# Six short blocks at the start, every load on one queue, and a new plan for a fused convolution and two-layer feed-forward kernel

## The chip, the cores and the metric

The kernel runs on one core of one Trainium2 chip. The metric is the device time of one execution in microseconds (us), as the median of several runs; smaller is better.

## The reference, cut to what matters

```
out[s] = sum_k softmax(weight_gen[s])[h, k] * x[s - 6 + k]       # 7 taps, 8 heads, 192 channels, zero padded
h  = out @ w_in1                                                  # 192 -> 2048
g  = (a0 + a1 h + a2 h^2 + a3 h^3) / (1 + |b0||h| + |b1| h^2)
x2 = g @ w_out1                                                   # 2048 -> 192
h  = x2 @ w_in2                                                   # 192 -> 2048
y  = (h * clip(h + 3, 0, 6) / 6) @ w_out2                         # 2048 -> 192
```

There are 8192 tokens (two sequences of 4096). The weights arrive as 64-bit floats and are turned into 32-bit ones on the chip.

## The kernel before, in words

**Tiling.** 128 partitions hold 128 runs of 64 consecutive tokens, so one row across the partitions is 128 tokens. A block is 256 tokens (2 rows) or 512 tokens (4 rows): `BL = [2, 2] + [4] * 15`. A unit `u` is two rows of convolution. For each block and each of 16 groups of 128 hidden columns, the kernel runs layer one, then layer two. A slice is 512 columns of one PSUM bank: one hidden group for a 512-token block, two for a 256-token block. There are 256 slices in all, 8 for a short block and 16 for a long one.

**Convolution.** Every four rows (a chunk) are loaded with their weights (`load_gen`, `load_chunk`), the softmax is done in five steps, and each row takes two multiplications (`conv_mul`, L177, on POOL) and two reductions (`conv_sum`, L192, on DVE). `x_dup`, `xT`, `x_hi` and `x_lo` transpose a unit on PE and split it in a high and a low part, so that two reduced-precision matmuls stand for one exact one.

**Layer one.** `in1` is five matmuls for each hidden group (L279). The function of h is then computed in one of two ways: a slice that is "whole" takes `act_v`, `act_s` (ACT) and `dve_q` (DVE, L321); the others take `act_u`, `act_w`, `act_q` (ACT) and `pool_q` (POOL, L341). `whole` is true for two slices of three. All slices share `act_l`, `dve_t`, `dve_t2`, `act_ln`, `act_exp`, `dve_hi`, `pool_m`, `dve_d` and `pool_lo`. `out1` (L418 to L422) adds five matmuls for each hidden group into `y1`, one tile of two PSUM banks for each block.

**Handover.** When `out1` of a block is complete, `mid_y`, `mid_f`, `mid_head`, `head_lo`, `mid_tail` and `tail_lo` fold and split `y1` into the input of layer two (`xh1`, `xl1`). The next block's first `out1` waits until `y1` is free again, that is, for `tail_lo` (L262).

**Layer two.** `in2` is five matmuls for each hidden group, `act_r2` and `dve_g2` follow, and `out2` (L454) is two or four rows of 16 matmuls each for the result, evacuated by `evac` and stored from SP's queue.

**Weights.** 28 jobs load a piece of a weight and decode it: `low`, `scale` (ACT), `join`, `sign` (DVE), `hi` (ACT) and `lo` (L532, mostly POOL). The first two jobs are loaded from ACT's queue, all others from SP's.

**The order.** `plan()` is a list scheduler in the kernel itself: every step has an engine, a cost, a due time and the steps it needs, and the order of each engine's instructions is what it returns. The due times come from the constants (`T`, `JP0`, `C1`, ...). Where the plan leaves PE idle ahead of the second block's layer two, it puts matmuls of the identity (`idle_mm`, L402), which compute nothing that is used.

Of the kernel before, what the change touches and what calls it, by code (L numbers as in the profile page):

```python
# [19 lines left out]
def kernel(  # L20
# [25 lines left out]
    BL = [2, 2] + [4] * 15  # L46
    B0 = [sum(BL[:b]) // 2 for b in range(len(BL))]
    BT = [n * P for n in BL]
    BV = [n // 2 for n in BL]
    BF = [GW // n for n in BT]  # L50
    BMAX = max(BT)
    UB = [(b, v) for b, n in enumerate(BV) for v in range(n)]
# [52 lines left out]

    def load_chunk(c):
        t = two.tile([P, ROWS, D], F32, tag="x", name="x")
        first = c * CT - (K - 1)
        neg = max(0, -first)
        cut_at = ROWS - 2 if c == 0 else ROWS  # L110
        segs = [(0, P, neg, cut_at)]
        if neg:
            for b in range(B):
                p = b * S // R
                nc.gpsimd.memset(t[p : p + 1, 0:neg, :], 0.0)
                segs += [(p + 1, p + 16, 0, neg), (p + 16, p + S // R, 0, neg)]
        if cut_at < ROWS:
            segs.append((0, P, cut_at, ROWS))
        for p0, p1, r0, r1 in segs:
            src = bass.AP(  # L120
                tensor=xf.tensor,
                offset=xf.offset + (first + p0 * R + r0) * D,
                ap=[[R * D, p1 - p0], [1, (r1 - r0) * D]],
            )
            nc.sync.dma_start(out=t[p0:p1, r0:r1].rearrange("p r d -> p (r d)"), in_=src)
        xch[c] = t
# [35 lines left out]
    NH = 4  # L162
    NS = 3
# [35 lines left out]
    def x_dup(u):  # L199
        t = xc[u]  # L200
        nc.scalar.activation(out=t[:, :, D:], in_=t[:, :, P:D], func=AF.Copy)

    def xT(u):
        t = xc.pop(u)
        ps = bank(("xT", u), [P, 2, HB], "xT")
        for s in range(2):
            nc.tensor.transpose(ps[:, 0, s * P : (s + 1) * P], t[:, s, 0:P], ident)  # L207
            nc.tensor.transpose(ps[:, 1, s * P : (s + 1) * P], t[:, s, P : 2 * P], ident)
        xps[u] = ps

    def x_hi(u):
        b, v = UB[u]
        if v == 0:
            xin[0, b] = [
                two.tile([P, 2, BMAX], F32R, tag=n, name=n)[:, :, : BT[b]] for n in ("xh0", "xl0")
            ]
        xh = xin[0, b][0]
        nc.scalar.activation(out=xh[:, :, v * HB : (v + 1) * HB], in_=xps[u], func=AF.Copy)

    def x_lo(u):  # L220
        b, v = UB[u]
        xh, xl = (t[:, :, v * HB : (v + 1) * HB] for t in xin[0, b])
        nc.vector.tensor_tensor(out=xl, in0=xps.pop(u), in1=xh.bitcast(F32), op=ALU.subtract)
# [3 lines left out]
    def mid_y(b):  # L227
        ysb[b] = one.tile([P, BMAX], F32, tag="ys", name="ys")[:, : BT[b]]
        for h in range(2):
            nc.scalar.activation(  # L230
                out=ysb[b][h * 64 : (h + 1) * 64],
                in_=y1[b][(1 - h) * 64 : (2 - h) * 64, 1, : BT[b]],
# [3 lines left out]
    def mid_head(b):  # L236
        n = BT[b]
        xin[1, b] = [
            one.tile([P, 2, BMAX], F32R, tag=t, name=t)[:, :, :n]
            for t in ("xh1", "xl1")  # L240
        ]
        nc.scalar.activation(out=xin[1, b][0][:, 0, :], in_=y1[b][:, 0, :n], func=AF.Copy)

    def head_lo(b):
        xh, xl = xin[1, b]
        nc.vector.tensor_tensor(
            out=xl[:, 0, :], in0=y1[b][:, 0, : BT[b]], in1=xh[:, 0, :].bitcast(F32),
            op=ALU.subtract,
        )

    def mid_f(b):
        c = y1[b][:, 1, : BT[b]]
        nc.vector.tensor_tensor(out=c, in0=c, in1=ysb.pop(b), op=ALU.add)

    def mid_tail(b):
        nc.scalar.activation(
            out=xin[1, b][0][:, 1, :], in_=y1[b][:, 1, : BT[b]], func=AF.Copy
        )

    def tail_lo(b):  # L260
        xh, xl = xin[1, b]
        nc.vector.tensor_tensor(  # L262
            out=xl[:, 1, :], in0=y1[b][:, 1, : BT[b]], in1=xh[:, 1, :].bitcast(F32),
            op=ALU.subtract,
        )

    def mm_in(i, xs, f, dst):
# [4 lines left out]
            (w["hi"], xh[:, 0, :]),  # L272
            (w["hi"], xl[:, 0, :]),
            (wst[i], xh[:, 1, :]),
            (wst[i], xl[:, 1, :]),
            (w["lo"], xh[:, 0, :]),
# [18 lines left out]
    def in1(sl):  # L295
        b, _ = SL[sl]
        h1[sl] = bank(("in1", sl), [P, GW], "h1")
        for i, n in enumerate(fs_of(sl)):
            mm_in(0, xin[0, b], n, cols(b, h1[sl], i))

    def whole(sl):
        return sl < QN and sl % QK in QS
# [89 lines left out]
    y1 = {}  # L392

    def open_y1(b):
        if b not in y1:
            y1[b] = ps_y.tile([P, 2, GW], F32, tag="y1", name="y1")

    def idle_mm(n):
        first = not y1
        open_y1(0)  # L400
        for i in range(n):
            nc.tensor.matmul(  # L402
                out=y1[max(y1)][:, i % 2, GW - P :], lhsT=ident, rhs=ident,
                start=first and i < 2, stop=False, skip_group_check=True,
            )

    def out1(sl):
        b, q = SL[sl]
        open_y1(b)
        a, c = y1[b][:, 0, : BT[b]], y1[b][:, 1, : BT[b]]  # L410
# [3 lines left out]
        for i, n in enumerate(fs_of(sl)):  # L414
# [5 lines left out]
            mm(out=c, lhsT=ws, rhs=gh, start=st, stop=False, **kw)  # L420
# [26 lines left out]
    def out2(b, v, part):  # L447
        if part == 0:
            y2[b, v] = bank(("out2", b, v, 0), [P, 2, D], "y2")
        for n in range(part * NF // 4, (part + 1) * NF // 4):  # L450
            q, i = divmod(n, BF[b])
            for s in range(2):
# [9 lines left out]
    def evac(b, v):  # L462
        u = B0[b] + v
        o = two.tile([P, 2, D], F32, tag="osb", name="osb")
        nc.scalar.activation(out=o, in_=y2.pop((b, v)), func=AF.Copy)
        nc.sync.dma_start(out=of[:, u * 2 : u * 2 + 2, :], in_=o)
# [106 lines left out]
    def job_step(key, n, e=None):  # L573
        eng = nc.vector if e == "DVE" else nc.gpsimd
        if n == "load":
            kind, a = key[0], key[1:]
            j = {"in": job_in, "pair": job_pair, "o1": job_out1, "o2": job_out2}[kind](*a)
            job_load(j, nc.scalar if key in order[:2] else nc.sync)
# [16 lines left out]
        else:  # L595
            for _, l in j["cuts"]:
                if l:
                    l(eng)
# [12 lines left out]
    CP = 0.946  # L611
    KP = 0.118
    WIN = 41.47
    SWL = 14.0
    BETA = 0.009
    C1 = -13.219
    CV = 3.155
    SM = 5.662
    XQ = -11.533
    XTP = 2.81  # L620
    XH = -3.719
    O1 = 4.488
    UM = 4.195
    I2 = -0.894
    SPR = 0.852
    R2 = -0.625
    O2 = 4.833
    OS = 0.939
    EV = 10.467
    IDLE = 0.2  # L630
    ops = {}
# [7 lines left out]
    def add(name, eng, cost, prio, fn, *a, after=(), take=(), lat=None):  # L639
# [8 lines left out]
    ]  # L648
    done = {}
    for n, key in enumerate(order):  # L650
        p = JP0 + min(n, 14) * JPT + max(0, n - 14) * JPU - (30.0 if n < 2 else 0.0)
        f64, split = WS == 2, key[0] != "o2"
        sz = 1.0 if key[0] in ("in", "pair") else 0.75
        last = ("job", key, "lo" if split else "sign" if f64 else "load")

        def step(k, eng, cost, prev, take=(), lat=None, also=[]):
            op(
                ("job", key, k), eng, cost, p - LP * (k == "load"), lambda e=None, key=key, k=k: job_step(key, k, e),
                ([("job", key, prev)] if prev else []) + also, take, lat,
            )  # L660

        flex = (("POOL", 1.25 * sz, 0.0), ("DVE", 0.62 * sz, PEN))
        step("load", "SP", 2.0 * sz, None, [("big", ST, [last])] if f64 or split else [], 2.0)
# [11 lines left out]
    for u, (b, v) in enumerate(UB):  # L675
        t0 = S0[b] * T - (BV[b] - 1 - v) * 8 * T
        c = u // 2
        if u % 2 == 0:
            t = t0 - CV * T
            add("gen", "SP", 0.6, t - XQ * T if c else X0P, load_gen, c, lat=2.0,  # L680
                take=[("wg", 2, [("softmax_m", c)])])
            add("load", "SP", 3.7, t - XQ * T + 1.0 if c else X0P + 0.5, load_chunk, c, lat=2.0,
                take=[("x", 2, [("conv_mul", 2 * c + 1, 1, 1)])])
            soft = (("POOL", 0.55, 0.0), ("DVE", 1.0, PEN))
# [5 lines left out]
                take=[("wk", 2, [("conv_mul", 2 * c + 1, 1, 1)])])  # L690
        for i in range(2):
# [257 lines left out]
```

## Time and profile before

| what | us |
|---|---|
| median of 3 runs | 1308.34 |
| lowest, highest | 1306.3, 1308.44 |
| the profiled execution, its own time | 1305.82 |
| its span in the trace | 1304.0 |
| PE busy in the span | 1281.1 |
| DVE busy | 1143.5 |
| ACT busy | 1069.3 |
| POOL busy | 984.3 |

The span lies inside the time of the execution, which is 1.8 us longer. PE is TensorE, DVE is VectorE, ACT is ScalarE, POOL is GpSimd, SP is SyncE, which only issues DMAs here. PE's busy time contains the identity matmuls of `idle_mm`.

### The profile page before, as it was taken

The page shows a single profiled execution, that of the slowest core. Times are in us where ns is not written, and L with a number is a line of the kernel's source. Part 1 is how long each engine was busy: PE and PEld are TensorE (multiplying, and loading weights), DVE is VectorE, ACT ScalarE, POOL GpSimd, SP SyncE. Part 2 cuts the span into 40 slices and gives each one's busy share as a digit, 9 for nine tenths or more (in the row PEclk, how much of TensorE's full clock was granted, in tenths as well). Part 3 has the DMA queues.
Part 4 walks back from the last instruction along what each step waited for, and adds up shares of the span by engine and source line. Part 5 has one row for each costly group of instructions (what it writes and reads, how often), then busy time and mean ns, then how long its engine had stood idle before and what let it go on. Part 6 is the DMA issues. An engine that isn't in the chain of part 4 may idle for free.

```text
span 1304.0 us, 18918 instructions
## 1 busy us (share of the span) xinstructions
PE 1281.1 (98%) x6640; PEld 1127.2 (86%) x6640; DVE 1143.5 (88%) x1774; ACT 1069.3 (82%) x1893; POOL 984.3 (75%) x811
## 2 busy tenths in 40 slices
PE   8889999999999999999999999999999999999998
PEld 8888878888889888898988889898888988888898
DVE  7899999999899898988989898898989889896931
ACT  6998989889788797978879798887979888797931
POOL 7998897978878787777968777787877778575620
PEclk9989999999999999999999999999999999999999
DMA  7440100110100101010010101001010000000000
GB/s 237 147 144 1 37 11 1 41 37 5 36 12 7 40 1 47 1 37 10 8 40 1 47 1 37 10 8 40 1 43 1 7 7 7 8 1 13 1 13 13
DMA packets 16263, 37.64 MB, mean 29 GB/s; under 512 B 1964, under 2 KB 12586, under 8 KB 16168
## 3 DMA queue, kind: packets, MB, share of 16 engines
q1 hardware_dynamic: 15864, 35.39, 8.3%
q10 hardware_dynamic: 304, 1.05, 0.3%
q8 instruction: 52, 0.85, 0.3%
q14 instruction: 43, 0.35, 0.1%
HBM read 30.14 MB, written 6.29 MB: 28 GB/s over the span
## 4 chain that ended last, share of the span: by engine, by line
PE 85%; ACT 7%; DVE 3%; POOL 2%; DMA 1%; issue 1%; SPq 0%; POOLq 0%; ACTq 0%
PE h L279 41%; PE y L454 24%; PE y L418 4%; PE y L421 4%; PE y L419 4%; PE y L420 4%; PE y L422 4%; ACT r L361 1%; ACT l L334 1%; ACT st L511 1%; ACT ys L230 1%; ACT r L356 1%; ACT w L316 1%; PE xT L207 1%; ACT v L311 1%
## 5 line engine op out<-in xcount | busy, mean ns | idle before, releaser
L389 POOL TENSOR_TENSOR glo<-w,r 128x512 fp32r<-128x512 f32 x256 | 331.0, 1295 | 186.5 <-PE y L422 113.5
L378 POOL TENSOR_TENSOR w<-w,ghi 128x512 f32<-128x512 f32 x256 | 330.9, 1295 | 44.1 <-DVE ghi L370 32.0
L454 PE MATMUL y<-wo,g 128*128 128x192 f32 x2048 | 352.1, 326 | 0.0
L454 PEld LDWEIGHTS y<-wo,g 128*128 128x128 f32 x2048 | 337.9, 190 | 8.5
L382 DVE SCALAR_TENSOR_TENSOR w<-h,acol,w 128x512 f32<-128x512 f32 x256 | 190.2, 744 | 34.1 <-POOL w L378 33.2
L437 ACT ACTIVATE g<-h 128x512 f32<-128x512 f32 x256 | 153.7, 600 | 71.1 <-PE h L279 69.0
L279 PE MATMUL h<-xh,wst 128*128 128x512 f32 (+1 forms) x544 | 206.1, 379 | 1.3 <-POOL wst L532 1.3
L279 PE MATMUL h<-xl,wst 128*128 128x512 f32 (+1 forms) x544 | 205.7, 378 | 0.1
L334 ACT ACTIVATE l<-h,acol 128x512 f32<-128x512 f32 x256 | 200.5, 783 | 2.5 <-PE h L279 2.5
L177 POOL TENSOR_TENSOR prod<-x,wk 128x672 f32<-128x672 f32 x127 | 189.4, 1503 | 17.3 <-DVE xc L192 12.1
L370 DVE SCALAR_TENSOR_TENSOR ghi<-h,acol,r 128x512 fp32r<-128x512 f32 x256 | 189.8, 744 | 10.9 <-PE y L420 3.9
L441 DVE SCALAR_TENSOR_TENSOR g<-g,h 128x512 f32<-128x512 f32 x256 | 174.1, 680 | 22.3 <-ACT g L437 20.7
L349 DVE SCALAR_TENSOR_TENSOR h<-l,acol,h 128x512 f32<-128x512 f32 x256 | 191.1, 749 | 2.4
L345 DVE TENSOR_TENSOR l<-h,l 128x512 f32<-128x512 f32 x256 | 174.0, 682 | 8.0 <-ACT l L334 4.7
L356 ACT ACTIVATE r<-w 128x512 f32<-128x512 f32 x256 | 161.2, 634 | 19.4 <-DVE w L321 15.3
L361 ACT ACTIVATE r<-r 128x512 f32<-128x512 f32 x256 | 161.7, 633 | 2.5
L321 DVE SCALAR_TENSOR_TENSOR w<-w,v 128x512 f32<-128x512 f32 x171 | 116.1, 679 | 22.3 <-ACT w L316 21.3
L311 ACT ACTIVATE v<-h,bab 128x512 f32<-128x512 f32 x171 | 112.9, 660 | 21.4 <-PE h L279 18.9
L316 ACT ACTIVATE w<-h,root 128x512 f32<-128x512 f32 x171 | 117.9, 690 | 7.8 <-DVE l L345 6.5
L279 PEld LDWEIGHTS h<-xh,wst 128*128 128x128 f32 x544 | 103.1, 189 | 20.8 <-POOL wst L532 1.5
L279 PEld LDWEIGHTS h<-xl,wst 128*128 128x128 f32 x544 | 102.9, 189 | 19.7 <-DVE xl L262 0.4
L341 POOL TENSOR_TENSOR w<-w,u 128x512 f32<-128x512 f32 x85 | 109.8, 1292 | 12.3 <-ACT w L327 10.6
(82 smaller groups left out, 2452.0 us busy)
## 6 DMA issues: line engine op xcount, KB each, us to landing
x<-in_x_dram SPq DMA_DIRECT2D x14, 960.0 KB, 4.7
st<-in_moe_w_out_dram SPq DMA_DIRECT2D x16, 384.0 KB, 3.3
out_dram<-osb SPq DMA_DIRECT2D x32, 192.0 KB, 1.8
st<-in_moe_w_in_dram SPq DMA_DIRECT2D x7, 512.0 KB, 4.7
wg<-in_weight_gen_dram SPq DMA_DIRECT2D x16, 112.0 KB, 2.0
st<-in_moe_w_in_dram SPq DMA_DIRECT2D x6, 256.0 KB, 4.1
x<-in_x_dram SPq DMA_DIRECT2D x1, 768.0 KB, 6.3
st<-in_moe_w_in_dram ACTq DMA_DIRECT2D x2, 256.0 KB, 5.7
```

Of the source, the lines that this page charges most:

```text
L177: eng.tensor_tensor(out=pr.rearrange("p (h g) k -> p k h g", g=G), in0=xch[c][:, t : t + K, hs].rearrange("p k (h g) -> p k h g", g=G), in ...
L279: nc.tensor.matmul(out=dst, lhsT=l[:, fs], rhs=r, start=(n == 0), stop=(n == len(seq) - 1), skip_group_check=True,)
L334: nc.scalar.activation(out=l, in_=h1[sl], func=AF.Identity, scale=acol[:, 3:4], bias=acol[:, 2:3])
L349: nc.vector.scalar_tensor_tensor(out=h, in0=e["l"], scalar=acol[:, 1:2], in1=h, op0=ALU.add, op1=ALU.mult)
L356: nc.scalar.activation(out=r, in_=e["w"], func=AF.Ln, bias=0.0 if whole(sl) else CEPS)
L361: nc.scalar.activation(out=r, in_=r, func=AF.Exp, scale=-1.0)
L370: nc.vector.scalar_tensor_tensor(out=ghi, in0=h, scalar=acol[:, 0:1], in1=e["r"], op0=ALU.add, op1=ALU.mult)
L378: nc.gpsimd.tensor_tensor(out=m, in0=m, in1=g1[sl][0].bitcast(F32), op=ALU.mult)
L382: nc.vector.scalar_tensor_tensor(out=m, in0=h1.pop(sl), scalar=acol[:, 0:1], in1=m, op0=ALU.add, op1=ALU.subtract)
L389: nc.gpsimd.tensor_tensor(out=glo, in0=e["m"], in1=e["r"], op=ALU.mult)
L441: nc.vector.scalar_tensor_tensor(out=g, in0=g, scalar=1.0, in1=h2.pop((b, q)), op0=ALU.min, op1=ALU.mult,)
L454: nc.tensor.matmul(out=y2[b, v][:, s, :], lhsT=g2[b, q][:, c : c + P], rhs=wo2[:, n, :], start=(n == 0 and s == 0), stop=(n == NF - 1), sk ...
```

## The change

- The first six blocks have 256 tokens, and 13 blocks of 512 follow (before: two and 15). Convolution units are tied to blocks through a table (`UB`, `UL`); blocks of 128 tokens become possible (`tight`) and are not used.
- All weight loads are issued from SP. The first two have due times of their own (`W0`), between the first load of `weight_gen` and the rest of the start: SP's queue begins with `weight_gen`, the first weight piece, the first chunk of x (three DMAs for six, the zeroes of the second sequence's edge written after the load), the second weight piece, the rest of x, the coefficients.
- `y1` is two tiles of one bank each (`ya`, `yc`), and `xh1`, `xl1` are two tiles each.
- The `lo` step of a decode is one step for each piece, and the matmuls wait for the pieces they read. `out2` waits for the `dve_g2` of its own slices instead of the last.
- `whole` is two of three for the first 48 slices and always after them.
- Three banks at most for layer one (`NH`, before four) and four for the rest (`NS`, before three).
- The planner's costs and constants are new.

```diff
-    BL = [2, 2] + [4] * 15
+    PRE = [2, 2, 2, 2, 2, 2]
+    BL = PRE + [4] * ((R - sum(PRE)) // 4)
...
+    def load_x(c, p0, p1, r0, r1):
+        first = c * CT - (K - 1)
+        src = bass.AP(
+            tensor=xf.tensor,
+            offset=xf.offset + (first + p0 * R + r0) * D,
+            ap=[[R * D, p1 - p0], [1, (r1 - r0) * D]],
+        )
+        to = xch[c][p0:p1, r0:r1].rearrange("p r d -> p (r d)")
+        nc.sync.dma_start(out=to, in_=src)
+
     def load_chunk(c):
...
+        if neg:
+            nc.gpsimd.memset(t[0:1, 0:neg, :], 0.0)
+            load_x(c, 16, P, 0, neg)
+            load_x(c, 1, 16, 0, neg)
+        load_x(c, 0, P, neg, ROWS if c else ROWS - 2)
+        for b in range(1, B if neg else 0):
+            nc.gpsimd.memset(t[b * P // B : b * P // B + 1, 0:neg, :], 0.0)
+
+    def load_rest():
+        load_x(0, 0, P, ROWS - 2, ROWS)
...
-    NH = 4
-    NS = 3
+    NH = 3
+    NS = 4
...
+    def rest(b, p):
+        xh, xl = (x[p] for x in xin[1, b])
+        nc.vector.tensor_tensor(out=xl, in0=y1[b][p], in1=xh.bitcast(F32), op=ALU.subtract)
...
     def whole(sl):
-        return sl < QN and sl % QK in QS
+        return sl % QK in QS if sl < QE else sl % QL in QT
...
+    def tight(b):
+        return BT[b] == P
 
     def open_y1(b):
-        if b not in y1:
-            y1[b] = ps_y.tile([P, 2, GW], F32, tag="y1", name="y1")
+        if b in y1:
+            return
+        n = BT[b]
+        if tight(b):
...
+        else:
+            ts = [ps_y.tile([P, GW], F32, tag=tag, name="y1") for tag in ("ya", "yc")]
+            y1[b] = [t[:, :n] for t in ts]
+            spare[b] = [t[:, GW - P :] for t in ts if n < GW]
...
-            job_load(j, nc.scalar if key in order[:2] else nc.sync)
+            job_load(j, nc.sync)
...
-    QN = 256
+    QE = 48
     QK = 3
     QS = [0, 1]
+    QL = 2
+    QT = [0, 1]
...
-    T = 4.254
+    T = 4.386
     X0P = -112.0
-    LP = 2.713
-    JP0 = 7.655
-    JPT = 2.744
+    W0 = [0.1, 0.7]
+    LP = 41.993
+    JP0 = 3.674
+    JPT = 3.06
     JPU = 2.458
-    PEN = 2.351
-    CP = 0.946
+    PEN = 7.306
+    CP = 0.031
...
-            step("lo", flex, 0, "hi")
+            for i, m in enumerate({"in": [512], "pair": [512, 512], "o1": [256, 128]}[key[0]]):
+                cp, cd = 0.06 + m * 0.00234, 0.08 + m / 960
+                step(i, (("POOL", cp, 0.0), ("DVE", cd + 0.2, PEN)), 0, "hi")
...
-                after = [("dve_g2", b, SN[b] - 1)] + [done["o2", 2 * p + j] for j in range(2)]
+                qs = range(SN[b]) if b >= OB else range(p * 4 // BF[b], (p * 4 + 3) // BF[b] + 1)
+                after = [("dve_g2", b, q) for q in qs] + done["o2", 2 * p] + done["o2", 2 * p + 1]
...
-            take=[("y1", 1, [("head_lo", b), ("tail_lo", b)])] if q == 0 else [])
+            take=[] if q else [("ya" if b % 2 == 0 else "yc", 1, [("head_lo", b), ("tail_lo", b)])]
+            if tight(b) else [("ya", 1, [("head_lo", b)]), ("yc", 1, [("tail_lo", b)])])
...
-    op(("coeffs",), "SP", 1.0, -70.0, coeffs, lat=3.0)
+    op(("coeffs",), "SP", 0.2, X0P + 1.2, coeffs, lat=3.0)
```

## Rows read from the trace of the kernel before

**Rows 1.** The page's first part: busy time of each engine.

```profile
span 1304.0 us, 18918 instructions
PE 1281.1 (98%) x6640; PEld 1127.2 (86%) x6640; DVE 1143.5 (88%) x1774; ACT 1069.3 (82%) x1893; POOL 984.3 (75%) x811
```

**Rows 2.** Stages by windows: from:to and length, busy us (instructions), granted clock, DMA.

```profile
0.00:20.00 20.00, 16.83 (x132) 16.40 (x133) 12.56 (x22) 9.38 (x18) 13.54 (x17) 1.00 0.88 250
20.00:80.00 60.00, 51.61 (x418) 48.74 (x416) 54.91 (x91) 57.50 (x116) 58.12 (x60) 1.00 0.53 169
80.00:120.00 40.00, 37.64 (x258) 34.64 (x259) 38.22 (x66) 38.55 (x73) 33.62 (x29) 0.92 0.17 52
120.00:205.00 85.00, 81.98 (x436) 72.09 (x436) 83.08 (x130) 76.22 (x137) 77.20 (x63) 0.98 0.06 19
205.00:1240.00 1035.00, 1032.54 (x5070) 899.03 (x5069) 937.02 (x1443) 871.52 (x1525) 795.05 (x640) 1.00 0.05 17
1240.00:1304.00 64.00, 60.54 (x333) 56.27 (x331) 17.71 (x26) 16.13 (x29) 6.78 (x6) 1.00 0.04 13
```

**Rows 3.** The same windows for line 402 alone (identity matmuls): PE, PEld.

```profile
0.00:20.00 20.00, 15.77 (x124) 15.50 (x124) 1.00 0.88 250
20.00:80.00 60.00, 25.76 (x212) 24.77 (x212) 1.00 0.53 169
80.00:120.00 40.00, 6.16 (x48) 5.79 (x48) 0.92 0.17 52
```

**Rows 4.** Timeline of ACT and its queue in the first 13 us.

```profile
3.63 1.85 ACTq L475 DMA_DIRECT2D st<-in_moe_w_in_dram  x3
12.07 0.20 ACT L796 ACTIVATE bab<-bcol 128x2 f32<-128x2 f32 x1 [8.05 <-DMA bcol<-in_moe_b_dram]
```

**Rows 5.** DMA issues by line: count, KB each, median us to landing.

```profile
st<-in_moe_w_in_dram ACTq DMA_DIRECT2D x2, 256.0 KB, 5.7
```

**Rows 6.** Timeline of the start: SP's queue, POOL, DVE, PE.

```profile
1.18 3.12 SPq L125 DMA_DIRECT2D x<-in_x_dram  x6
1.30 2.15 POOL L115 MEMSET x<- 1x1152 f32 x2
7.57 1.39 DVE L177 TENSOR_TENSOR prod<-x,wk 128x672 f32<-128x672 f32 x1 [2.05 <-DMA x<-in_x_dram]
19.14 0.36 PE L279 MATMUL h<-xh,win0hi 128*128 128x256 f32 x1
```

**Rows 7.** Timeline of PE around the start of block 2.

```profile
100.30 2.17 PE L402 MATMUL y<-ident 128*128 128x128 f32 x18
...
106.27 0.50 PE L279 MATMUL h<-xh,win0hi 128*128 128x512 f32 x1 [1.12 <-DVE xl L223]
```

**Rows 8.** Timeline of PE, where block 3 takes over the output bank.

```profile
196.10 0.79 PE L418 MATMUL y<-ghi,wo1h 128*128 128x512 f32 x1 [2.30 <-DVE xl L262]
```

**Rows 9.** The same place by windows.

```profile
194.00:197.00 3.00, 0.90 (x2) 0.80 (x3) 3.00 (x5) 2.27 (x4) 2.59 (x3) 0.78 0.00 0
```

**Rows 10.** Timeline of PE: starts of 256-column matmuls that follow each other.

```profile
88.05 0.28 PE L419 MATMUL y<-ghi,wo1l 128*128 128x256 f32 x1
88.17 0.28 PE L420 MATMUL y<-ghi,wo1s 128*128 128x256 f32 x1
```

**Rows 11.** The chain that ended last: start, us, 512-column matmuls.

```profile
290.03 3.40 PE h L279 x15
```

**Rows 12.** Groups by line: busy us, mean ns, idle before, releaser.

```profile
L321 DVE SCALAR_TENSOR_TENSOR w<-w,v 128x512 f32<-128x512 f32 x171 | 116.1, 679 | 22.3 <-ACT w L316 21.3
L341 POOL TENSOR_TENSOR w<-w,u 128x512 f32<-128x512 f32 x85 | 109.8, 1292 | 12.3 <-ACT w L327 10.6
```

**Rows 13.** Timeline of DVE: what one such step occupies between neighbours.

```profile
57.24 0.68 DVE L321 SCALAR_TENSOR_TENSOR w<-w,v 128x512 f32<-128x512 f32 x1
57.84 0.74 DVE L382 SCALAR_TENSOR_TENSOR w<-h,acol,w 128x512 f32<-128x512 f32 x1
```

**Rows 14.** Windows of one long block's period in the middle.

```profile
511.00:587.50 76.50, 76.50 (x378) 66.84 (x378) 69.53 (x107) 64.31 (x113) 59.25 (x49) 1.00 0.05 19
```

**Rows 15.** Waits of DVE from 205 to 1240: us in total, times, longest.

```profile
DVE w L382 <- POOL w L378: 28.7, 44, 1.5
DVE w L321 <- ACT w L316: 20.6, 19, 2.4
```

More of the change, by code (lines that the diff above doesn't have):

```diff
@@ L104, in load_gen @@
         wgt[c] = g
[L106 to L126 removed]
+    def load_x(c, p0, p1, r0, r1):
[7 more added lines that the diff above has]
+        nc.sync.dma_start(out=to, in_=src)
+    def load_chunk(c):
+        t = xch[c] = two.tile([P, ROWS, D], F32, tag="x", name="x")
+        neg = max(0, K - 1 - c * CT)
+        if neg:
+            nc.gpsimd.memset(t[0:1, 0:neg, :], 0.0)
[6 more added lines that the diff above has]
+        load_x(0, 0, P, ROWS - 2, ROWS)
     mxs = {}
@@ L400, in idle_mm @@
         open_y1(0)
-        for i in range(n):
+        to = spare[max(y1)]
+        for i in range(n if to else 0):
             nc.tensor.matmul(
-                out=y1[max(y1)][:, i % 2, GW - P :], lhsT=ident, rhs=ident,
-                start=first and i < 2, stop=False, skip_group_check=True,
+                out=to[i % len(to)], lhsT=ident, rhs=ident,
+                start=first and i < len(to), stop=False, skip_group_check=True,
             )
@@ L419, in out1 @@
             mm(out=a, lhsT=wo1l[:, n, :], rhs=gh, start=False, stop=False, **kw)
-            mm(out=c, lhsT=ws, rhs=gh, start=st, stop=False, **kw)
+            mm(out=c, lhsT=ws, rhs=gh, start=st and not tight(b), stop=False, **kw)
             mm(out=a, lhsT=wo1h[:, n, :], rhs=gl, start=False, stop=sp, **kw)
@@ L451, in out2 @@
             q, i = divmod(n, BF[b])
-            for s in range(2):
+            for s in range(min(2, BL[b])):
                 c = i * BT[b] + v * HB + s * P
@@ L689 @@
             add("softmax_m", soft, 0, t - SM * T + 4.0, softmax_m, c, after=[("softmax_b", c)],
-                take=[("wk", 2, [("conv_mul", 2 * c + 1, 1, 1)])])
-        for i in range(2):
+                take=[("wk", 2, last_mul(c))])
+        for i in range(nt):
             for z in range(2):
@@ L726 @@
             f = (q + 1) * BF[b] - 1
-            jobs_in = [done["in", 1, f // 4], done["pair", 1, f // 8 * 2]]
+            jobs_in = [k for n in range(q * BF[b], f + 1)
+                       for k in done["in", 1, n // 4] + done["pair", 1, n // 8 * 2]]
             add("in2", "PE", cm, t2, in2, b, q, lat=0.2,
@@ L748 @@
         last = fs_of(sl)[-1]
-        jobs_in = [done["in", 0, last // 4], done["pair", 0, last // 8 * 2]]
-        c = 5 * BF[b] * (0.0137 + BT[b] / 2400)
+        jobs_in = [k for n in fs_of(sl) for k in done["in", 0, n // 4] + done["pair", 0, n // 8 * 2]]
+        jobs_out = [k for n in fs_of(sl) for k in done["o1", n // 2]]
+        c = 5 * BF[b] * (0.0137 + max(BT[b], 234) / 2400)
         add("in1", "PE", c, t, in1, sl, lat=0.2,
-            after=[("x_lo", B0[b] + v) for v in range(BV[b])] + jobs_in
+            after=[("x_lo", u) for u, k in enumerate(UB) if k[0] == b] + jobs_in
             + ([("in1", sl - 1)] if sl else []),
@@ L756 @@
             add("act_v", "ACT", 0.57, t + 1.1 - C1, act_v, sl, after=[("in1", sl), ("bab",)],
-                take=[("s", NS, [("dve_q", sl)])])
-            add("act_s", "ACT", 0.57, t + 1.6 - C1, act_s, sl, after=[("in1", sl), ("root",)],
-                take=[("w", NB["w"], [("pool_lo", sl)])])
-            add("dve_q", "DVE", 0.661, t + 2.3 - C1, dve_q, sl, after=[("act_v", sl), ("act_s", sl)])
+                take=[("s", NS, [("dve_q", sl)]), ("w", NB["w"], [("pool_lo", sl)])])
+            add("act_s", "ACT", 0.57, t + 1.6 - C1, act_s, sl,
+                after=[("in1", sl), ("root",), ("act_v", sl)])
+            add("dve_q", "DVE", 0.6, t + 2.3 - C1, dve_q, sl, after=[("act_v", sl), ("act_s", sl)])
         else:
@@ L905 @@
         when = {o["key"]: (t0, t1) for o, _, t0, t1 in steps}
-        fold = [(when["mid_y", b][0], when["tail_lo", b][1]) for b in range(2)]
+        fold = [
+            (when["mid_y", b][0], when["tail_lo", b][1]) for b in range(len(BL)) if BT[b] < GW
+        ]
         last = 2.0
```

186 lines of the change are left out of this document (95 added, 91 removed), and 5 rows, old and new, of the table order.

## The prediction

> **What bounds the kernel now.** I read the busy times first. PE is busy for 1281.1 of 1304.0 us [rows 1], but that contains the identity matmuls. So I cut the span into stages [rows 2] and looked at line 402 alone in the same stages [rows 3]. What PE loses in a stage is its idle time plus the time of line 402:
>
> - 0 to 20: 3.2 idle + 15.8 identity = 18.9 us
> - 20 to 80: 8.4 + 25.8 = 34.2 us
> - 80 to 120: 2.4 + 6.2 = 8.5 us, and the granted clock is 0.92
> - 120 to 205: 3.0 us, clock 0.98
> - 205 to 1240: 2.5 us of 1035
> - 1240 to the end: 3.5 us, the last evacuation and store
>
> That is 70.6 us, and 61.6 of them lie ahead of 120. From 205 on PE is the bound, and no plan can take more than 2.5 us out of those 1035. The reader should see in [rows 2] what bounds the first 120 us instead: from 20 to 80 ACT is busy for 57.5 of 60, POOL for 58.1, DVE for 54.9. They decode weights and do layer one of two short blocks, and PE gets only what they finish. The identity matmuls fill the rest.
>
> **The start.** ACT does nothing from 4 to 12.07, where it waits for the coefficients, which left SP behind the x loads; the first weight piece had been issued from ACT's own queue at 3.63 and lands in 5.7 us, so at about 9.4 [rows 4, 5]. With the change this piece is second on SP's queue, at about 1.2, and at the same 5.7 us it lands at about 7, and the plan puts its decoding ahead of the coefficients. That gives ACT up to 12.1 - 7 = 5 us of work earlier, if the wait for the coefficients (still late on SP) is behind it. Against it: x now stands behind 512 KB, about 2.0 us at the 250 GB/s of the first stage [rows 2], so the first multiplication moves from 7.57 to about 9.6; and one of the two zero fills (2.15 us for two, so 1.1 each) now follows the load instead of preceding it [rows 6]. The first real matmul, at 19.14 [rows 6], needs both; the convolution path gets 3 us later and the weight path 5 us earlier. The ends are +3 (x decides) and -5 (ACT decides). I take -3, nearer to ACT, since ACT is the fullest from there to 80. Three DMAs leave ACT's sequencer (1.85 us [rows 4]) and join SP's, where three x issues go away; I cost that exchange at nothing, hidden while SP is ahead of the data; without that cover it is 1.85 us.
>
> The trace has the DMA engines 0.88 busy in this stage [rows 2], so they are what is shared. The Trainium skill, DMA: Bandwidth & Descriptors, section Issuing engines are not separate DMA queues, says that a second issuing engine saves only the time of issuing. By it, giving up ACT's queue costs at most those 1.85 us, and the sum would move by no more.
>
> **Short blocks in the first 200 us.** Block 2 is long now, so its first matmul waits for four rows of convolution: PE runs 18 identity matmuls from 100.30 and then stands 1.12 us until `x_lo` is done at 106.27 [rows 7]. A 256-token block 2 needs half of those rows, so it can begin earlier, and layer-two work of blocks 1 and 2 follows in smaller portions. What can come back is at most the loss of 80 to 120, 8.5 us plus the slow clock (8% of 40, 3.2 us), and a little of 20 to 80, where ACT has only 2.5 us free: so 0 to -14. I take -8, since the elementwise engines that are full ahead of 80 stay full.
>
> Handover: block 3 waits 2.30 us for `tail_lo` [rows 8], and the clock falls to 0.78 there after PE was busy for only 0.90 of 3 us [rows 9]. With two tiles the first two matmuls need `head_lo` alone, one DVE step earlier. But the same 1536 tokens now have six handovers where they had four. A stall like that one with its slow clock is about 2.3 + 0.7 = 3 us: ends -3 (gone) and +6 (two more of them). I take -1.
>
> Width: neighbouring 256-column matmuls start 0.12 us apart [rows 10], and 15 of 512 columns take 3.40, so 0.2267 each [rows 11]. Four more short blocks have 4 x 16 x 15 = 960 narrow matmuls in place of 480 wide ones: 115.2 - 108.8 = +6.4 us of PE time. While PE runs identity matmuls that is free, so the ends are 0 and +6.4; blocks 2 to 5 lie mostly behind 105, where PE has little left to fill. I take +5.
>
> The Trainium skill, TensorE: Matmul & The Clock Gate, section Back-to-back issue gap, gives N/2.4 + 2.5 ns for columns N, so 109.2 and 215.8 ns. By it the width would cost 104.8 - 103.6 = 1.2 us, and the sum would be about 5 us lower. The trace disagrees and decides: 120 and 226.7.
>
> **The slices in the middle.** 171 slices are whole now [rows 12]; after, 32 of the first 48 and all other 208, so 240, which is 69 more. Each moves a step to DVE that occupies 0.60 us [rows 13] and takes 1.29 us off POOL [rows 12]: DVE +41, POOL -89. In a long block's period of 76.5 us, DVE is busy for 69.5 [rows 14]; 16/3 x 0.60 = 3.2 more gives 72.7. POOL and ACT have room to spare and get more. PE does the same work. So I cost it at nothing, with DVE's 7 us of idle time as the cover; the ends are -2.5 (PE's stalls of the middle go) and the price of the rival below. I take -1, for the shorter chain of a slice.
>
> **Edits at nothing.** The split of `xh1`, the decode's `lo` by pieces and `out2`'s own slices only remove waits. Layer one with three banks instead of four could hold `in1` back: before, PE idled 2.5 us in all in the middle [rows 2], whatever the cause; I keep +3 as an upper end. Of the last 64 us PE is busy in 60.5 [rows 2], in the order of the code, so the end stays. The new constants have no row; what they can win in the start is the 0 to -14 above. I take a further -2 for the 20 to 80 stage, out of ACT's 2.5 us of idle time there.
>
> **Sum.** -3 - 8 - 1 + 5 - 1 - 2 = -10 on the span of 1304.0, so 1294, and 1.8 us around it: 1296. The profiled execution is 2.5 us below the median of the runs; I put half of that on top and say **1297 us**.
>
> **Rivals.**
>
> *A, DVE becomes the bound in the middle (slower).* DVE's 72.7 leave 3.8 us in a period. Its two largest waits, for `pool_m` and for `act_s`, are 28.7 and 20.6 us in 1035 [rows 15]. The second grows by half as `dve_q` does, to 31; together 60 in 13.5 periods, 4.4 each. If they stay, a period is 77.1; with DVE's smaller waits, which bring its present idle time to 7 us a period [rows 14], it is up to 79.7. The middle between is +1.9 on 13 periods, +25 us, and with the gains of the start 1294 + 25 + 3 = about 1320; at the low end 1305. It decides from 3.8 us of waits in a period. For it: DVE is already busy for 83 of 85 us from 120 to 205 [rows 2]. Against it: these waits exist while PE sets the pace, and an engine that is late waits less. Chance 0.17.
>
> *B, the start gains more.* If layer two of block 0 comes well ahead of 80, PE has work while ACT decodes. The loss of 20 to 80 is 34 us; a third of it, 11 us, on top of the sum: 1286. For it: a layer-two slice gives PE as much as a layer-one slice and needs two elementwise steps instead of ten. Against it: ACT and POOL have 2 us free there, and the decode steps are the same. Chance 0.18.
>
> *C, the gains are eaten.* The narrow matmuls cost their 6.4, two more handovers stall at 3 us each, the start gains 5 to 10: 1304 + 6 + 6 - 8 = 1308 on the span at most, 1304 to 1311 as a time. For it: six handovers, three banks. Against it: the split tiles. Chance 0.18.
>
> *The forecast,* 1289 to 1304, has 0.47.
>
> **How the numbers follow.** A difference under 0.2% (2.6 us, so 1305.7 to 1311.0) is about what a measurement of this kernel can't tell from no change. Faster: 0.47 + 0.18, of A and C nearly nothing: 0.65. Same: most of C, 0.13 with A's low end. Slower: 0.22, the rest of A and C. The range leaves out B's better half and A's upper half: 1282 to 1314; the likeliest case alone is 1289 to 1304.
>
> **What would show it.** The first layer-one matmul ahead of 19.14 and ACT's first decode near 7: the start. Identity matmuls worth less than 47.7 us, and PE less idle from 80 to 205: the short blocks. Starts 0.12 apart up to about 250 us: the width. From about 250 to 1240 a period of 76.5 us, DVE busy for about 72.7 of it, PE idle under 3 us: the middle. The prediction is wrong if the period grows by more than 0.3 us, if PE stalls at the handovers of the short blocks, or if ACT still waits for the coefficients ahead of its first decode.

## The result and the profile after

The changed kernel takes 1295.45 us (median of 5 runs, 1295.3 to 1296.44) against 1306.71 us for the kernel before beside it. The ratio is 0.9915, with a 95% interval of 0.9901 to 0.9928: 11 us faster. The profiled execution took 1295.45 us, 1293.7 of them in the span.

The stages by windows, as in [rows 2] (from:to, length, then busy us of PE, PEld, DVE, ACT, POOL with counts, granted clock, DMA share, GB/s):

```profile
0.00:20.00 20.00, 16.83 (x129) 16.59 (x130) 12.06 (x20) 9.11 (x18) 13.33 (x16) 1.00 0.84 255
20.00:80.00 60.00, 52.60 (x424) 50.55 (x423) 55.23 (x92) 58.60 (x118) 56.66 (x60) 0.98 0.49 151
80.00:120.00 40.00, 38.89 (x296) 37.88 (x295) 39.42 (x66) 39.42 (x74) 33.76 (x28) 0.99 0.16 50
120.00:205.00 85.00, 84.81 (x662) 84.22 (x662) 83.98 (x137) 76.70 (x140) 74.78 (x62) 1.00 0.08 23
205.00:1230.00 1025.00, 1025.00 (x5258) 903.33 (x5257) 980.34 (x1513) 842.90 (x1461) 718.27 (x577) 1.00 0.05 18
```

And the same windows for the identity matmuls alone (now line 414), as in [rows 3]:

```profile
0.00:20.00 20.00, 16.34 (x125) 16.25 (x126) 1.00 0.84 255
20.00:80.00 60.00, 26.64 (x214) 25.15 (x212) 0.98 0.49 151
80.00:120.00 40.00, 2.71 (x20) 2.49 (x20) 0.99 0.16 50
```

Ahead of 80 nothing has moved: PE idles or runs identity matmuls for 19.5 and 34.0 us, before 18.9 and 34.2. From 80 to 120 that falls from 8.5 to 3.8 us, from 120 to 205 from 3.0 to 0.2, and from 205 to 1230 PE has no idle time left (before, from 205 to 1240, 2.5).

Busy time hides slow matmuls, so for all comparisons below I count what PE loses in another way: the length of a stage minus what its matmuls need at the distance at which they follow each other. That is 0.2267 us for 512 columns, 0.12 for 256 [rows 10, 11], 0.1627 for one of `out2` (16 of them take 2.60 us in the traces, which makes 0.1625; the difference is 0.3 us in the last column, in every version alike), 0.11 for a transpose; the identity matmuls count as loss. The width term of the narrow matmuls is then no loss but part of the need. The table has all versions; its fourth column is the start of the first layer-one matmul.

| version | median us | span us | first matmul at | lost 0 to 80 | 80 to 205 | 205 to 1200 |
|---|---|---|---|---|---|---|
| before | 1306.7 | 1304.0 | 19.1 | 54.7 | 18.7 | 5.4 |
| after | 1295.5 | 1293.7 | 20.1 | 54.4 | 6.0 | 1.9 |
| before, six short blocks | 1323.4 | 1320.2 | 19.3 | 55.0 | 18.5 | 15.0 |
| before, all slices whole | 1327.5 | 1325.4 | 20.0 | 54.4 | 26.9 | 17.5 |
| after, two short blocks | 1304.7 | 1302.9 | 22.8 | 55.9 | 19.5 | 2.3 |
| after, four | 1304.3 | 1302.0 | 20.5 | 53.2 | 16.8 | 3.5 |
| after, twelve | 1306.0 | 1304.1 | 22.7 | 54.3 | 7.7 | 0.9 |
| after, two of three whole | 1296.4 | 1294.6 | 20.8 | 54.5 | 6.7 | 1.7 |
| after, output bank pair as one tile | 1316.2 | 1314.7 | 21.5 | 55.1 | 9.3 | 19.1 |
| after, first weights from ACT | 1296.2 | 1294.8 | 21.4 | 54.9 | 6.6 | 1.8 |
| after, start rearranged | 1305.1 | 1303.4 | 23.2 | 53.6 | 15.1 | 2.8 |
| after, old constants | 1300.6 | 1298.1 | 20.2 | 55.1 | 7.2 | 4.6 |
| after, DVE step reading SBUF added | 1415.9 | 1413.2 | 22.2 | 54.2 | 6.8 | 108.2 |
| after, DVE step reading PSUM added | 1329.2 | 1327.8 | 22.6 | 54.6 | 7.0 | 33.3 |

The table also shows what one trace can't tell. Four of its versions run the changed kernel's instructions in the changed kernel's order, at least up to 260 us, and differ from it only further on or in a tile: two of three whole, the pair as one tile, and both with an added step. Their first matmul is at 20.8, 21.5, 22.2 and 22.6 us, where the changed kernel's is at 20.1. Without the one with the tile, they lose 6.7 to 7.0 us from 80 to 205, where the changed kernel loses 6.0. A start that differs by 2.5 us, or a loss that differs by 1, is therefore not yet the work of an edit.

The bookkeeping closes: from before to after the losses fall by 78.8 - 62.3 = 16.5 us and 960 narrow matmuls add 6.4, so -10.1 against -10.3 in the spans.

### The profile page after: what moved, and what is told of

Same layout as the page of the kernel before. It is cut to its first block, busy times and chain, and to the rows that moved or that the text cites. A ratio compares the mean times of both kernels' runs of the same rounds, so it can differ in the third digit from the quotient of the medians.

```text
span 1293.7 us, 19782 instructions
## 1 busy us (share of the span) xinstructions
PE 1278.5 (99%) x7092; PEld 1148.9 (89%) x7092; DVE 1188.2 (92%) x1848; ACT 1042.5 (81%) x1832; POOL 902.4 (70%) x743
## 4 chain that ended last, share of the span: by engine, by line
PE 90%; ACT 5%; POOL 2%; DVE 2%; issue 1%; DMA 0%; SPq 0%; POOLq 0%; ACTq 0%; DVEq 0%
PE h L275 43%; PE y L466 25%; PE y L433 4%; PE y L431 4%; PE y L430 4%; PE y L432 4%; PE y L434 4%; ACT st L523 1%; ACT l L331 1%; POOL prod L181 1%; ACT dt L519 1%; ACT r L353 0%; PE xT L213 0%; PE xT L212 0%; ACT r L358 0%
## 5 line engine op out<-in xcount | busy, mean ns | idle before, releaser
L466 PE MATMUL y<-wo,g 128*128 128x192 f32 x2048 | 352.2, 326 | 0.0
L466 PEld LDWEIGHTS y<-wo,g 128*128 128x128 f32 x2048 | 337.0, 190 | 7.3
L275 PE MATMUL h<-xh,wst 128*128 128x512 f32 (+1 forms) x608 | 216.8, 357 | 0.0
L275 PE MATMUL h<-xl,wst 128*128 128x512 f32 (+1 forms) x608 | 216.7, 356 | 0.0
L308 ACT ACTIVATE v<-h,bab 128x512 f32<-128x512 f32 x240 | 157.6, 657 | 55.0 <-PE h L275 52.2
L453 DVE SCALAR_TENSOR_TENSOR g<-g,h 128x512 f32<-128x512 f32 x256 | 174.1, 680 | 19.7 <-ACT g L449 17.2
L318 DVE SCALAR_TENSOR_TENSOR w<-w,v 128x512 f32<-128x512 f32 x240 | 163.0, 679 | 14.9 <-ACT w L313 11.3
L313 ACT ACTIVATE w<-h,root 128x512 f32<-128x512 f32 x240 | 164.1, 684 | 0.0
L275 PEld LDWEIGHTS h<-xl,wst 128*128 128x128 f32 x608 | 115.1, 189 | 16.8
L275 PEld LDWEIGHTS h<-xh,wst 128*128 128x128 f32 x608 | 115.1, 189 | 16.5
L275 PE MATMUL h<-xh,win0hi 128*128 128x512 f32 (+1 forms) x304 | 117.0, 385 | 1.5 <-DVE w L379 1.5
```

The costliest lines, as they stand in the source:

```text
L275: nc.tensor.matmul(out=dst, lhsT=l[:, fs], rhs=r, start=(n == 0), stop=(n == len(seq) - 1), skip_group_check=True,)
L313: nc.scalar.activation(out=w, in_=h1[sl], func=AF.Square, scale=root[:, 3:4])
L453: nc.vector.scalar_tensor_tensor(out=g, in0=g, scalar=1.0, in1=h2.pop((b, q)), op0=ALU.min, op1=ALU.mult,)
L466: nc.tensor.matmul(out=y2[b, v][:, s, :], lhsT=g2[b, q][:, c : c + P], rhs=wo2[:, n, :], start=(n == 0 and s == 0), stop=(n == NF - 1), sk ...
```

## The experiments

Every version below has its order planned anew from its own code, unless it says otherwise, so one edit also shifts its neighbours. In four of them the traces show the changed kernel's order on every engine: the output bank pair as one tile, the first weights from ACT's queue, and both added steps. The ratio is always to the kernel before, run on the same chip.

### Six short blocks alone, in the kernel before

```diff
-    BL = [2, 2] + [4] * 15
+    BL = [2] * 6 + [4] * 13
```

> The kernel before with six blocks of 256 tokens and 13 of 512, its old constants kept and its order planned anew from them. Theory (the short blocks give PE work from 80 to 205): this edit alone wins most of what the whole change wins there, 13 us, and pays 6 us for narrow matmuls; 1298 to 1302 us, 0.4 to 0.8% faster, PE's loss from 80 to 205 falls from 19 to under 10 us. Rival (the new constants and the split tiles won it): the narrow matmuls alone show, 1310 to 1314 us, and the loss from 80 to 205 stays over 15 us.

1323.36 us, ratio 1.0129 (1.0113 to 1.0144): slower by 17 us. Both expectations fail. The loss from 80 to 205 stays, as the rival said, but 10 us of new loss appear behind 205, and 6.4 of width come on top. Short blocks alone do not win.

### All slices whole, in the kernel before

```diff
-    QK = 3
+    QK = 2
```

> The kernel before with every one of its 256 slices whole, 85 more than before. Theory (DVE has room in the middle, but is full ahead of 205): the period of a long block stays 76.5 us with DVE near 73; the first 205 us get slower by up to 16 more DVE steps of 0.6 us, so 1308 to 1316 us. Rival (DVE becomes the bound in the middle): the period grows to 77 us or more, over 1316 us. Rival (a shorter chain without POOL helps): under 1304 us.

1327.53 us, ratio 1.0160 (1.0146 to 1.0173). PE loses 8 us more from 80 to 205 and 12 more from 205 to 1200, so the period of the middle grows by 0.9 us in the mean, and the time is in the range of the first rival. But its reason isn't there. Windows from 300 to 1200:

```profile
300.00:1200.00 900.00, 889.90 (x4369) 773.44 (x4368) 840.39 (x1301) 721.63 (x1247) 610.20 (x492) 1.00 0.05 17
```

DVE is busy for 840.4 of 900 us, which is less than the 857.5 of the changed kernel (below), where PE is full. So DVE is not the bound here. PE's waits in this stretch are 6.2 us for `tail_lo` at handovers and 3.9 for `dve_g2` ahead of transposes; which edit of the order would take them away is open.

### Two and four short blocks, in the changed kernel

```diff
-    PRE = [2, 2, 2, 2, 2, 2]
+    PRE = [2, 2]
```

> The changed kernel with only two blocks of 256 tokens and 15 of 512, all else kept. Theory (short blocks): the losses from 80 to 205 come back to 13 to 19 us from 6, and 6 us of narrow matmuls go: 1299 to 1304 us, slower than the changed kernel by 4 to 8. Rival (constants and split tiles won it): only the 6 us of width show, 1288 to 1291 us, faster than the changed kernel.

> The changed kernel with four short blocks and 14 long ones. Theory (two short blocks cost 3.3 us of narrow matmuls where PE is full and win what PE loses from 120 to 205 without them, some 3 to 7 us of the 8.1 that the version with two loses there): between the changed kernel and 1299 us. Rival (the loss is over after four): 1291 to 1293 us, faster than the changed kernel.

With two, 1304.69 us, ratio 0.9987 (0.9978 to 0.9996); with four, 1304.28, ratio 0.9984 (0.9975 to 0.9992). The version with two lost 19.5 us from 80 to 205, over the upper end of the theory's 13 to 19, and its time came out a little over the expected 1299 to 1304. The version with four (the same edit with `[2] * 4`) fell on neither side: it keeps 16.8 of that loss.

### Twelve short blocks

```diff
-    PRE = [2, 2, 2, 2, 2, 2]
+    PRE = [2] * 12
```

> The changed kernel with twelve blocks of 256 tokens, so 10 of 512. Theory (narrow matmuls cost what their starts show, 0.12 us against half of 0.2267, wherever PE is full): six more blocks cost 6 x 1.6 = 9.6 us, 1303 to 1307 us. Rival (by the isolated gap of a page, 109.2 and 215.8 ns): 1.8 us, 1296 to 1298. Rival (more short blocks help the start further): under 1295.

1305.98 us, ratio 0.9996 (0.9987 to 1.0005). Six more short blocks cost 10.5 us, 1.75 each, against 1.6 from the starts of the matmuls. The three losses together grow by only 0.6 us, so nearly all of it is width where PE is full, and the theory stands.

### Two slices of three whole all the way

```diff
-    QL = 2
+    QL = 3
```

> The changed kernel with two slices of three whole all the way, as before the change. Theory (whole slices moved work from POOL and ACT to DVE, neither of which PE waits for in the middle): the same time within 2 us, 1293.5 to 1297.5, DVE busy for 71 of 76.5 us in a long block's period instead of 74.4. Rival (the shorter chain of a whole slice removed PE's stalls in the middle): 1298 us or more, with PE idle again for 2 us or more from 205 to 1230.

1296.36 us, ratio 0.9920 (0.9907 to 0.9934), 0.9 us from the changed kernel. Windows from 300 to 1200 of this version, and of the changed kernel below it:

```profile
300.00:1200.00 900.00, 900.00 (x4450) 786.95 (x4449) 828.85 (x1261) 768.90 (x1330) 698.15 (x557) 1.00 0.05 18
```

```profile
300.00:1200.00 900.00, 900.00 (x4449) 786.81 (x4448) 857.54 (x1320) 733.17 (x1267) 624.21 (x501) 1.00 0.05 18
```

PE is full in both. Making the other slices whole put DVE from 828.9 to 857.5 of 900 us and won nothing that can be measured.

### The output bank pair as one tile

```diff
-            ts = [ps_y.tile([P, GW], F32, tag=tag, name="y1") for tag in ("ya", "yc")]
+            t2 = ps_y.tile([P, 2, GW], F32, tag="y1", name="y1")
+            ts = [t2[:, i, :] for i in range(2)]
...
-            if tight(b) else [("ya", 1, [("head_lo", b)]), ("yc", 1, [("tail_lo", b)])])
+            if tight(b) else [("ya", 1, [("head_lo", b), ("tail_lo", b)])])
```

> The changed kernel with layer one's output as one tile of two banks again, which the next block takes when both its parts are free. Theory (the split saves the handovers' stalls): each of the six short handovers stalls PE for 0.5 to 1.5 us, 1298 to 1303 us, and PE idles again where the first out1 matmul of a block waits for tail_lo. Rival (the short blocks always leave PE other work at a handover): the same time within 2 us.

1316.16 us, ratio 1.0071 (1.0059 to 1.0084): 21 us slower than the changed kernel, and the place is another than the theory's. PE's waits from 300 to 1200 (waiting line, releaser: us in total, times, longest):

```profile
PE y L431 <- DVE xl L248: 13.8, 12, 1.3
```

The changed kernel has no wait of PE in that stretch. The stall is at twelve handovers of long blocks, 1.15 us each, not at the short ones. It waits for `tail_lo`, which the first matmul of the next block needs only because both banks are one tile. The order of the instructions is the changed kernel's on every engine, so this is the price of the one tile in that order. The kernel before has one tile and no such stall in the middle, in its own order, where the due time of the handover steps (`UM`) is another; whether that is why was not tested.

### The first weights from ACT's queue

```diff
-            job_load(j, nc.sync)
+            job_load(j, nc.scalar if key in order[:2] else nc.sync)
```

> The changed kernel with the first two weight jobs issued from ACT's queue again, the order of all steps kept. Theory (the start is decided by the path of x: landing, zero fill, softmax product): x no longer stands behind the weights on SP and loses at most 1 us, so 1294 to 1297 us, the first layer-one matmul between 18.5 and 20.5 us. Rival (the earlier weight load pays): the decode starts later than 6.4 us and the time grows by 2 us or more.

1296.18 us, ratio 0.9918 (0.9904 to 0.9931), 0.7 us from the changed kernel. In the same order of steps the queue is worth nothing here, and the prediction's upper end of 1.85 us holds. The first matmul came at 21.4, not by 20.5, which is inside the spread of the changed kernel's order.

### The start rearranged

```diff
-            nc.gpsimd.memset(t[0:1, 0:neg, :], 0.0)
-            load_x(c, 16, P, 0, neg)
-            load_x(c, 1, 16, 0, neg)
+            for b in range(B):
+                p = b * P // B
+                nc.gpsimd.memset(t[p : p + 1, 0:neg, :], 0.0)
+                load_x(c, p + 16, p + P // B, 0, neg)
+                load_x(c, p + 1, p + 16, 0, neg)
...
-        for b in range(1, B if neg else 0):
-            nc.gpsimd.memset(t[b * P // B : b * P // B + 1, 0:neg, :], 0.0)
...
-            add("softmax_m", soft, 0, t - SM * T + 4.0, softmax_m, c, after=[("softmax_b", c)],
+            add("softmax_m", soft if c else (("DVE", 0.6, 0.0),), 0, t - SM * T + 4.0, softmax_m if c else (lambda c, e="DVE": softmax_m(c, e)), c, after=[("softmax_b", c)],
...
-    op(("coeffs",), "SP", 0.2, X0P + 1.2, coeffs, lat=3.0)
+    op(("coeffs",), "SP", 1.2, X0P - 1.0, coeffs, lat=3.0)
```

> The changed kernel with three edits of the start: both zero fills ahead of the loads again (five DMAs for the first chunk of x instead of three), the first chunk's softmax product always on DVE, and the coefficients first on SP's queue. Theory (the start is 1 us later than before because x waits for the fill and the product, and ACT waits 1.2 us for the coefficients and 3.2 for what follows them): the first layer-one matmul goes from 20.1 to 17 to 19 us and the time to 1292 to 1295 us. Rival (ACT, DVE and POOL are full from 20 to 80 us, so an earlier first matmul changes nothing): the same time within 1 us though the first matmul is earlier.

1305.12 us, ratio 0.9988 (0.9979 to 0.9997): slower by 9.7 us than the changed kernel, and both expectations fail. The coefficients are there at 4.7 us, but x lands 3 us later and the first matmul is at 23.2. That costs nothing ahead of 80, where the loss is 53.6. What it lost comes from 80 to 205, 15.1 us against 6.0: block 2 begins at 112.6 instead of 107.2, PE runs 54 identity matmuls from 80 to 120 instead of 20, and stands for up to 2.2 us at a time for layer two's `dve_g2` (L453). An edit of the first ten microseconds gave the whole plan another order: the matmuls of PE, without the identity ones, come in another order from 49 us on.

### The old constants

```diff
-    T = 4.386
+    T = 4.254
...
-    C1 = -8.144
+    C1 = -13.219
...
-    UM = 10.223
+    UM = 4.195
...
```

> The changed kernel with 23 of the planner's constants as before the change (the due times T, LP, JP0, JPT, C1 to EV, and the penalties PEN, CP, KP, WIN, SWL); six short blocks, split tiles, whole slices and the planner's new costs are kept. Theory (structure and constants belong together, as the kernel before lost 17 us by six short blocks alone): slower than the changed kernel by 10 us or more, 1305 us or over. Rival (short blocks and split tiles carry the gain whatever the constants): 1293 to 1299 us.

1300.60 us, ratio 0.9957 (0.9945 to 0.9970). It lies between the two. With the old constants the new structure has 1.2 us more loss from 80 to 205, hardly more than the spread of one order, and 2.7 more behind it; with all else changed, the 23 constants are worth 5 of the 11 us.

### DVE's room in the middle, measured by one more step

The first version adds a step whose operands are both in SBUF, the second one that reads PSUM. Nothing reads either, and the order is that of the changed kernel.

```diff
+        if sl >= QE:                                   # first version, behind dve_q
+            nc.vector.tensor_tensor(
+                out=extra, in0=e["w"][:, :P], in1=e["w"][:, :P], op=ALU.add
+            )
...
+        if sl >= QE:                                   # second version, behind dve_t2
+            nc.vector.tensor_scalar_mul(extra, h[:, :P], 0.5)
```

> The changed kernel with one more DVE addition of 128 x 128 (0.2 us) in each slice after the first 48, which nothing reads, in an unchanged order: 16 for each long block, 3.3 us. Theory (DVE is busy for 74.4 of 76.5 us in a period and has 2 us left): the period grows by about 1.2 us in 13 periods, 1308 to 1316 us, and DVE is the full engine in the middle, with PE idle for over 10 us there. Rival A's point (waits of 4 us or more stay in each period whatever DVE has to do): the period grows by all of 3.3 us, over 1330 us. Rival (DVE has more room than its busy time shows): the same time within 3 us.

> The same test of DVE's room in the middle with another addition: in each slice after the first 48, one more DVE multiplication of 128 x 128 that reads PSUM instead of SBUF and that nothing reads, in an unchanged order, placed behind the second polynomial step. Theory one (the 0.71 us that the former addition took, with both operands in SBUF, came from sharing with POOL; DVE's room is 2 us in a period): this one takes about 0.2 us, 3.3 us in a period, and the kernel is slower by 10 to 25 us than the changed one, 1305 to 1320 us. Theory two (the former addition was slow for its place in the order): again over 0.5 us each and over 1380 us. Rival (DVE has more room than its busy time shows): within 3 us of the changed kernel.

The first took 1415.88 us, ratio 1.0834 (1.0820 to 1.0849), the second 1329.16, ratio 1.0176 (1.0162 to 1.0190). All instructions of the added step in the first version, and in the second (duration in ns, least, median, greatest):

```profile
L323 DVE TENSOR_TENSOR extra<-w x208: 291/881/1452, 262.0 to 1352.1; 128x128 f32<-128x128 f32 x104
```

```profile
L351 DVE TENSOR_SCALAR extra<-h x208: 290/291/293, 265.4 to 1267.6; 128x128 f32<-128x128 f32 x104
```

The first step was no measure of room, because its length was another than assumed; what made it long is in the last section. The second is a measure. Its windows from 300 to 1200:

```profile
300.00:1200.00 900.00, 885.38 (x4296) 756.30 (x4295) 876.58 (x1473) 712.67 (x1231) 613.20 (x492) 1.00 0.05 18
```

PE now waits (8.5 of 14.0 us for `pool_lo`, the rest for DVE), and DVE stops at 876.6 of 900 us, 97.4%: if it is DVE that sets the pace here, 23.4 us of idle time remain even so, which is 2.0 in 76.5 us. In the changed kernel DVE is busy for 857.5 / 900 x 76.5 = 72.9 us of a period. So an estimate from this one version is that 76.5 - 72.9 - 2.0 = 1.6 us were free, not the 3.6 that the busy time shows. The version is 33.7 us slower than the changed kernel, 2.6 in each of 13 periods: more than the 10 to 25 us that the first theory has for a period near full, and less than the 3.3 of a period in which nothing of the step is hidden (16 steps, each 0.208 us from its start to that of the next one; busy they are for 0.29, so 3.3 is a low measure).

## Why the prediction was right

The forecast of 1297 us lies 1.5 us from the result, and the chosen case came, none of the three rivals. The sum was right with terms that were not.

**The start: -3 forecast, nothing measured.** This step failed. The first weight piece did land early, and ACT decodes it at 6.4 instead of 12.2. Timeline of the start after the change (start, us, engine, line; in brackets idle time and releaser):

```profile
6.39 0.69 ACT L523 ACTIVATE st<-st 128x512 int32<-128x512 uint32 x1 [2.38 <-DMA st<-in_moe_w_in_dram]
...
7.94 1.05 POOL L127 MEMSET x<- 1x1152 f32 x1 [5.59 <-DMA x<-in_x_dram]
...
9.08 0.59 POOL L156 TENSOR_TENSOR wk<-ex,sg 128x224 f32<-128x224 f32 x1
...
9.71 1.42 DVE L181 TENSOR_TENSOR prod<-x,wk 128x672 f32<-128x672 f32 x1 [0.66 <-POOL wk L156]
...
16.34 0.20 ACT L838 ACTIVATE root<-root 128x1 f32<-128x1 f32 x1 [3.20 <-DVE root L835]
...
20.11 0.36 PE L275 MATMUL h<-xh,win0hi 128*128 128x256 f32 x1
```

x landed at 7.9, only 0.4 us later than before [rows 6]. In the nine traces with these first loads it lands 0.4 to 1.8 us later, so the 2.0 that I added for the weights ahead of it is an upper end. The zero fill then cost its 1.05, and the softmax product, which the new plan gives to POOL behind the fill, another 0.6, so the first multiplication came at 9.71, close to the 9.6 of the forecast by other terms. ACT gained nothing: it did its decode early and stood 3.2 us for the coefficients' chain, which DVE had put behind convolution and decode steps. ACT was busy for 9.1 us of the first 20, before 9.4 [rows 2]. More important, the step asked the wrong question. In the fourteen versions of the table the first matmul is anywhere from 19.1 to 23.2 us, and what PE has lost by 80 is 53.2 to 55.9 without following it.

**20 to 80: -2 forecast, -0.3 for 0 to 80 in all.** ACT did fill its idle time, from 57.5 to 58.6 us busy, with no gain for PE. Rival B had no part in it: line 275's first matmul of layer two is at 78.6, before at 80.1.

**80 to 205: -8 for short blocks and -1 at the handovers forecast, -12.7 measured.** The stage was right, the size was low, and the step behind the -8 failed. 8.3 of the gain (13.2 - 4.9) lie from 80 to 120, as forecast, and 4.5 from 120 to 205, where I had valued the handover at one. But block 2, which was to begin earlier, begins at 107.2, where it began at 106.3 [rows 7]. What fills the stage is `out2`: 48 of its matmuls run from 80 to 120, 7.8 us of work, where there was one. PE and DVE before (`dve_g2` is L441, `out2` L454):

```profile
119.04 0.68 DVE L441 SCALAR_TENSOR_TENSOR g<-g,h 128x512 f32<-128x512 f32 x1
119.78 5.47 PE L454 MATMUL y<-wo,g 128*128 128x192 f32 x32
```

And after (`dve_g2` is L453, `out2` L466):

```profile
91.49 2.77 PE L466 MATMUL y<-wo,g 128*128 128x192 f32 x16
...
107.22 0.36 PE L275 MATMUL h<-xh,win0hi 128*128 128x256 f32 x1
...
120.11 0.68 DVE L453 SCALAR_TENSOR_TENSOR g<-g,h 128x512 f32<-128x512 f32 x1
```

These two `dve_g2` are the last of block 0. Before, `out2` of the block waits for it; after, it begins 28 us ahead of that step, with the slices that are done. That is the edit to `out2`'s wait, which I had put among those at nothing. No version takes this edit alone back, so its worth is not measured. It isn't enough by itself: the versions with two and four short blocks have 32 and 36 of these matmuls by 120 and still lose 19.5 and 16.8 us from 80 to 205.

The stall of [rows 8] is gone, and so is the fall of the clock from 120 to 205: 1.00 after 0.98. What else carries the gain is less clear than the forecast had it. Seven of the eight versions with six or twelve short blocks and split tiles in the new planner lose 6.0 to 7.7. But the eighth, with a rearranged start, loses 15.1 with the same six blocks in another order, so the losses with two and four blocks can be their order's too. And six short blocks in the kernel before lose 18.5, so short blocks are not enough by themselves. What has to come with them is neither the split of the output bank pair alone (as one tile in the new planner: 9.3) nor the 23 constants alone (the old ones in the new structure: 7.2). Beside `out2`'s wait, the four tiles of layer two's input, the load order, the numbers of banks and the planner's rules were not separated.

**Width: +5 forecast, +6.4 by count.** The twelve blocks give 1.75 us for each short block, so 7.0 for four; without the 0.6 us of loss that came with them it is 6.5. The trace's distances hold. The gap of the Trainium skill, TensorE: Matmul & The Clock Gate, section Back-to-back issue gap, by which six more short blocks would cost 1.8 us, does not fit this kernel; the section gives that formula for a single isolated matmul, so it was no rule for this stream. (By it the sum would have been 4 us lower, not 5, since 5 was what I had taken.)

**The middle: -1 forecast, -3.5 measured** (5.4 to 1.9 from 205 to 1200). DVE's busy time came out at 72.9 us a period where 72.7 was forecast. But whole slices did not win it: with two of three the loss is 1.7 all the same. It comes with the new order; with the old constants it is 4.6. The prediction had 2.5 us as the most that the middle could give, which is PE's idle time there. That ceiling was wrong: 5.4 us were lost, because PE counts as busy in part of what it loses.

**Edits at nothing.** Splitting the output bank was costed as a wait removed. It is that, and the new order would lose 21 us without it, at the long handovers. `out2`'s own slices filled the stage from 80 to 120. For the three banks of layer one the prediction kept +3 as an end; no run tests them, and PE has no wait left in the middle.

**Rival A** was nearer than its 0.17 suggests. It decides from 3.8 us of waits that stay in a period; by the added step 2.0 stay, so the changed kernel stands an estimated 1.6 us short of that edge. The kernel before with all slices whole did not go over it: its DVE was busy for 840.4 of 900 us.

The five misses are +3 at the start, +1.7 ahead of 80, +1.4 of width, and -3.7 and -2.5 in the two later stages, which nearly cancel. That the time came out is in part luck: the term of -8 was filled by work that the prediction had not counted.

## What to carry to other kernels

Where one engine waits for three others that are full, find what it loses by stage and by need, not by busy time; between versions the first matmul here moved by 4 us, and what PE had lost by 80 us by less than 3. When a stage gains, count the work that fills it by kind: here it was that of a step whose wait had been cut from the last slice to its own. A plan, its block sizes and the tiles it may release one by one belong together: any of them alone can cost what together they win, so an edit to a planned kernel is judged with the order planned for it, and a change of 9 us may be the order's. The room of DVE was smaller here than its idle time; add a small step to it and see where the time begins to grow.

## What the runs showed of the hardware

A DVE step of 128 x 128 with both operands in SBUF takes 0.29 us by itself and up to 1.45 beside POOL. Timelines of DVE and of POOL in the first version with an added step:

```profile
629.14 1.02 DVE L323 TENSOR_TENSOR extra<-w 128x128 f32<-128x128 f32 x1
```

```profile
628.64 1.50 POOL L182 TENSOR_TENSOR prod<-x,wk 128x672 f32<-128x672 f32 x1
```

This step begins inside POOL's multiplication and ends with it, at 630.16 and 630.14. Of 170 such steps from 300 to 1200, 164 began inside an instruction of POOL and took 0.74 us in the mean; 138 of these ended 0.14 to 0.16 us after that instruction, and 21 within 0.04 us of its end. The other six took 0.29 each. The multiplication of the same size with one input, from PSUM, took 0.290 to 0.293 in all 208, of which 164 began inside an instruction of POOL. And in the first version's own trace `dve_q`, with one input from SBUF and one from PSUM, took 0.68 us in the mean inside an instruction of POOL (155 times) and outside (85) alike. The Trainium skill, SBUF — State Buffer, section Who interferes with whom, says that a DVE instruction with two SBUF inputs contends with a GpSimd instruction that reads SBUF, and one with at most one SBUF input, outside DVE's two-port modes, does not. These rows agree.
